# Moving the later attention loads to GpSimd's queue and attention's result copies and stores to ScalarE

## The chip, the cores and the metric

The kernel runs on one core of one Trainium2 chip. The metric is the device time of one execution in microseconds, the median of several runs. The kernel before has 885.93 us (three runs, 885.02 to 886.97).

## What is computed

Attention with fixed masks, then two chains of matrix products over its 2304 rows:

```python
# q, k, v: 4 batches x 8 heads x 576 positions x 64, float32
scores = (q @ k^T) / 8
# heads 0-3: a key counts if 0 <= i - j < 32
# heads 4-7: a key counts if 0 <= i - j < 128 and (i - j) % 4 == 0
attn = softmax(where(mask, scores, -1e9))
x  = (attn @ v) laid out as 2304 x 512
y  = ((x @ w1) * (x @ w2)) @ w3 @ w_out          # 512 -> 1024 -> 1024 -> 512
z  = (silu(y @ w_gate) * (y @ w_val)) @ w_out2    # 512 -> 1536 -> 512
```

## The kernel before

**Pairs and units.** The 8 heads of a batch are taken two at a time, so there are 16 pairs, four to a batch (pair 0 to 3 is batch 0). A pair's attention is seven units: `scores(i, g)` for two halves of its nine blocks of 64 queries (matmuls L319, mask L333, maximum L336, exponentials on ScalarE L338, normalisation L341 to L343 on VectorE), `transposes(i, g)` for three groups of blocks (L356, copied out of PSUM by ScalarE, L358), and `values(i, g)` for two halves (L371). The halves of a pair use two PSUM banks, `bk6` and `bk7`, once the first weights are folded.

**Loads of a pair.** `load_q` (L296, two DMAs), `load_k` (L299) and `load_v` (L304) bring a pair's inputs. q and k have two buffers: those of pair i+2 are issued when `scores(i, 1)` is done. v has one buffer: that of pair i+1 is issued when `values(i, 1)` is done. In the kernel before, SyncE (SP) issues all of them.

**Weights.** A block of two weight tiles, 1 MB, is loaded by SP into one of three raw buffers (`raw<-w_in`, L155), turned into float32 by ScalarE (L200) and VectorE (L201, L202), and split into a high and a low part (L195 on ScalarE, L196 on VectorE). A raw buffer can be loaded again when L196 has read it. From chunk 0 on, weights of the last stage are converted in the same way by `quarters()` (L514, L515), and stored by SP to DRAM as `wd` and `wod` (L552).

**Chunks.** The first chain works on five chunks of rows (512, 512, 512, 512, 256). Chunk 0 takes attention's result of batch 0 straight from PSUM (L164, L165). The others are read back from DRAM: `values` of pairs 4 to 15 copies its two halves into an output buffer `o0` or `o1`, the first half with ScalarE (L394), the second with VectorE (L396), and SP stores it to `x1d` (L397). The chunk is then loaded as a 1 MB block (`raw<-x1d`, also L155) and split (L164, L165). Inside a chunk, `gate_a` (bank `bk4`, copied to `ta` by L236), `gate_b` (bank `bk5`, L242, split into `p`) and `contract` (banks `bk0` to `bk3`) run for eight slices, and `drain` copies the four banks out (L259 on ScalarE, L261 on VectorE, the same buffers `o0` and `o1`) and stores them from ScalarE's queue (`x2d<-o`, L262). Attention of batch c+1 is spread among the slices of chunk c. All matmuls of a product come as three, L217 to L219 (high by high, high by low, low by high). After chunk 4 comes the last stage (from about 437 us), which has no attention in it.

**Order.** A scheduler decides where the instructions of these pieces stand on each engine from the program and its own estimate of durations; on an engine they then run in that order, and so do the DMAs of one queue.

The lines that decide which queue and engine is used are these:

```python
nc.sync.dma_start(out=ks[i % 2][:, WIN:], in_=k_in[i])                   # load_k, L299
nc.vector.tensor_copy(place(o), src)                                     # second half of a pair's result, L396
nc.sync.dma_start(out=x1d[hp, :, b * S:(b + 1) * S], in_=o)              # its store, L397
```

Of the kernel before, what the change touches and what calls it, by code (L numbers as in the profile page):

```python
# [14 lines left out]
AF = mybir.ActivationFunctionType  # L15
# [3 lines left out]
B, H, S, D = 4, 8, 576, 64  # L19
# [5 lines left out]
WIN = 32  # L25
DIL = 4
NPAIR = H // 2
NP = B * NPAIR
QB = 64
KW = QB + WIN  # L30
# [58 lines left out]
def moe_chain_kernel(tc, q_in, k_in, v_in, w_in, mask_in, out):  # L89
    nc = tc.nc  # L90
# [7 lines left out]
    with static as st, other as ot, psum as pp, dram as dp:  # L98
# [14 lines left out]
        x1d = dp.tile([KT, P, NT], F32, name="x1d")  # L113
# [7 lines left out]
        i = N_W1  # L121
# [41 lines left out]
        def to_parts(src, hi, lo):  # L163
            nc.scalar.activation(hi, src, AF.Copy)  # L164
            return nc.vector.tensor_tensor(out=lo, in0=src, in1=hi.bitcast(F32), op=ALU.subtract)  # L165
# [106 lines left out]
        with att1_pool as a1, att2_pool as a2:  # L272
# [3 lines left out]
            ks = [a1.tile([P, WIN + S], F32, name=f"k{i}") for i in range(2)]  # L276
            vv = a1.tile([P, NBLK, P], F32, name="v")
# [10 lines left out]
            def q_halves(q, j):  # L288
                h = slice(j * D, (j + 1) * D)
                z = q[h].rearrange("d (n z r) -> d n z r", z=2, r=2 * QB)  # L290
                return h, z[:, :, j], z[:, :, 1 - j]

            def load_q(i):
                for j in range(2):
                    h, dst, _ = q_halves(qd[i % 2], j)
                    nc.sync.dma_start(out=dst, in_=q_in[i, h].rearrange("d (n r) -> d n r", r=2 * QB))  # L296

            def load_k(i):
                nc.sync.dma_start(out=ks[i % 2][:, WIN:], in_=k_in[i])  # L299

            def load_v(i):
                src = v_in[i]
                win = bass.AP(tensor=src.tensor, offset=src.offset, ap=[[P, KW], [QB * P, NBLK], [1, P]])
                nc.sync.dma_start(out=vv[:KW], in_=win)  # L304


            att_banks = batt + acc[2:]
# [1 line left out]
            def att_bank():  # L309
                count["att"] += 1  # L310
                return att_banks[count["att"] % len(att_banks)]

            def scores(i, g):
# [33 lines left out]
                if g == 1:  # L347
                    if i + 2 < NP:
                        load_q(i + 2)
                        load_k(i + 2)  # L350
# [9 lines left out]
            def values(i, g):  # L360
                b, hp = divmod(i, NPAIR)

                half = S // 2 if hp >= NPAIR // 2 else 5 * QB
                a, e = (0, half) if g == 0 else (half, S)
                ps = att_bank()
                for n in range(NBLK):
                    lo, hi = max(n * QB, a), min((n + 1) * QB, e)
                    if lo >= hi:
                        continue
                    for j in range(2):  # L370
                        nc.tensor.matmul(  # L371
                            ps[j * D:(j + 1) * D, lo - a:hi - a],
                            vv[:KW, n, j * D:(j + 1) * D],
                            pt[:KW, n, (j + n) % 2 * QB + lo - n * QB:(j + n) % 2 * QB + hi - n * QB],
                            start=True, stop=True,
                        )
                src = ps[:, :e - a]
                if hp >= NPAIR // 2:
                    src = src.rearrange("p (c j) -> p c j", c=2)

                    def place(t):
                        return t.rearrange("p (j c) -> p c j", c=DIL)[:, 2 * g:2 * g + 2]
                else:

                    def place(t):
                        return t[:, a:e]

                if b:

                    if g == 0:  # L390
                        count["o"] += 1
                    o = ost[count["o"] % len(ost)]
                    if g == 0:
                        nc.scalar.activation(place(o), src, AF.Copy)  # L394
                    else:
                        nc.vector.tensor_copy(place(o), src)  # L396
                        nc.sync.dma_start(out=x1d[hp, :, b * S:(b + 1) * S], in_=o)  # L397
                elif hp >= NPAIR // 2:
                    cut = CMAX // DIL
                    parts = [xb[0][:, w, hp].rearrange("p (j c) -> p c j", c=DIL)[:, 2 * g:2 * g + 2] for w in range(2)]  # L400
                    to_parts(src[:, :, :cut], *parts)
                    nc.vector.tensor_copy(xr.rearrange("p (j c) -> p c j", c=DIL)[:, 2 * g:2 * g + 2], src[:, :, cut:])
                else:
                    cut = min(e, CMAX)
                    to_parts(src[:, :cut - a], *[xb[0][:, w, hp, a:cut] for w in range(2)])
                    if e > cut:
                        nc.vector.tensor_copy(xr, src[:, cut - a:])
                if b == 0 and g == 1:
                    nc.sync.dma_start(out=x1d[hp, :, CMAX:S], in_=xr)
                if g == 1 and i + 1 < NP:  # L410
                    load_v(i + 1)
# [3 lines left out]
            for i in range(NP):  # L415
                if i + 1 < NP:
                    units += [(scores, i + 1, g) for g in range(2)]
                units += [(transposes, i, g) for g in range(3)]
                units += [(values, i, g) for g in range(2)]
                done_at.append(len(units))  # L420
# [22 lines left out]
            for kk in ks:  # L443
                nc.gpsimd.memset(kk[:, 0:WIN], 0.0)
            make_identity(nc, ident)
            load_k(0)
            load_q(0)
            load_block()
            nc.sync.dma_start(out=mask[:, :2], in_=mask_in[:, :2])
            load_block()  # L450
            load_k(1)
            load_q(1)
            load_v(0)
            load_block()
            nc.sync.dma_start(out=mask[:, 2:], in_=mask_in[:, 2:])
# [8 lines left out]
            for s in range(2 * K1):  # L464
                h, j = divmod(s, K1)
# [386 lines left out]
```

## Time and profile before

| what | us |
|---|---|
| median of three runs | 885.93 |
| the profiled execution's own time | 883.1 |
| its span, first to last instruction | 881.3 |
| TensorE (PE) matmuls busy | 850.6, 97% of the span |
| VectorE (DVE) busy | 595.5, 68% |
| ScalarE (ACT) busy | 350.5, 40% |
| GpSimd (POOL) busy | 3.2 |

The span is what the profiler shows instruction by instruction; the time of the execution is 1.8 us longer. An idle time is listed with the engine and line that ended it. Matmul ends are modelled, so that a matmul's listed duration overlaps the next one's. "SPq" and "ACTq" are the instructions by which an engine issues a DMA. The granted clock of TensorE (PEclk) is given as a share of 2.4 GHz.

### The profile page before, as it was taken

The numbers are of one execution on the slowest core, as the hardware profiler recorded it, in microseconds if no ns is written. First come the engines' busy times: TensorE is split into PE (matmuls) and PEld (weight loads), VectorE is DVE, ScalarE is ACT, GpSimd is POOL, SyncE is SP. The second block draws the span as 40 slices with busy tenths as digits, with TensorE's granted clock in tenths as the row PEclk, the third lists the DMA queues.
The fourth block names the chain that finished last, engine by engine and source line by source line (L and its number), as shares of the span: only waits on it lengthen the run. The fifth ranks groups of instructions, "written<-read, shape, count | busy, mean of one in ns | idle before, by whom it ended". The sixth has DMA issues, their size and how long they took to land.

```text
span 881.3 us, 13296 instructions
## 1 busy us (share of the span) xinstructions
PE 850.6 (97%) x5065; PEld 774.9 (88%) x5066; DVE 595.5 (68%) x1105; ACT 350.5 (40%) x809; POOL 3.2 (0%) x12
## 2 busy tenths in 40 slices
PE   7699899979999999999899999999999999999998
PEld 5478788857888788888899999999999999999998
DVE  6788957447645672465667776798766686666666
ACT  5786854445544552444453222242222132222221
POOL 1000000000000000000000000000000000000000
PEclk9799999989999999999999999999999999999999
DMA  9988738574874667467799666678766667766312
GB/s 282 266 279 273 251 117 267 168 239 124 277 227 141 220 210 262 159 206 248 245 369 372 215 211 201 196 269 263 226 205 214 203 205 248 241 205 213 120 48 73
DMA packets 92432, 192.95 MB, mean 219 GB/s; under 512 B 6480, under 2 KB 56272, under 8 KB 87632
## 3 DMA queue, kind: packets, MB, share of 16 engines
q1 hardware_dynamic: 89488, 187.37, 65.2%
q10 hardware_dynamic: 2880, 4.72, 1.5%
q8 instruction: 40, 0.66, 0.3%
q14 instruction: 24, 0.20, 0.1%
HBM read 150.65 MB, written 41.42 MB: 218 GB/s over the span
## 4 chain that ended last, share of the span: by engine, by line
PE 50%; DMA 13%; DVE 4%; ACT 3%; issue 2%; SPq 0%; ACTq 0%; DVEq 0%
PE bk L217 17%; PE bk L219 17%; PE bk L218 17%; DMA raw<-w_in 6%; DMA wd<-stage 3%; DMA wd<-mid 1%; DMA raw<-x1d 1%; DMA x1d<-o 1%; DVE mid L515 1%; DVE stage L515 1%; DVE x L165 1%; ACT mid L514 1%; ACT s L338 1%; DVE p L165 0%; ACT raw L200 0%
## 5 line engine op out<-in xcount | busy, mean ns | idle before, releaser
L705 DVE TENSOR_TENSOR s<-bk,s 128x384 f32<-128x384 f32 x252 | 137.7, 554 | 52.4 <-PE bk L219 31.5
L217 PE MATMUL bk<-x,w 128*128 128x512 f32 (+2 forms) x368 | 137.3, 374 | 7.6 <-ACT x L164 3.9
L218 PE MATMUL bk<-x,w 128*128 128x512 f32 (+2 forms) x368 | 136.7, 372 | 0.1
L219 PE MATMUL bk<-x,w 128*128 128x512 f32 (+2 forms) x368 | 136.0, 369 | 0.0
L219 PE MATMUL bk<-p,wo 128*128 128x384 f32 x288 | 97.3, 338 | 0.0
L217 PE MATMUL bk<-p,wo 128*128 128x384 f32 x288 | 96.8, 337 | 0.0
L218 PE MATMUL bk<-p,wo 128*128 128x384 f32 x288 | 96.8, 336 | 0.0
L747 DVE TENSOR_TENSOR acc<-bk,acc 128x384 f32<-128x384 f32 x120 | 66.5, 554 | 44.7 <-PE bk L219 44.3
L708 ACT ACTIVATE s<-s 128x384 f32<-128x384 f32 x72 | 37.6, 525 | 129.0 <-DVE s L705 127.9
L217 PEld LDWEIGHTS bk<-x,w 128*128 128x128 f32 x368 | 70.1, 191 | 18.3 <-ACT ta L236 4.6
L218 PEld LDWEIGHTS bk<-x,w 128*128 128x128 f32 x368 | 70.5, 192 | 9.9 <-DVE x L165 0.5
L219 PEld LDWEIGHTS bk<-x,w 128*128 128x128 f32 x368 | 70.5, 191 | 9.8
L164 ACT ACTIVATE p<-s 128x384 fp32r<-128x384 f32 x72 | 37.7, 526 | 101.6 <-DVE s L709 101.6
L217 PE MATMUL bk<-w 128*128 128x384 f32 (+1 forms) x196 | 70.7, 365 | 3.9 <-ACT w L195 3.9
L218 PE MATMUL bk<-w 128*128 128x384 f32 (+1 forms) x196 | 70.3, 360 | 0.0
L218 PE MATMUL bk<-w,mid 128*128 128x384 f32 x204 | 68.6, 336 | 0.0
L200 ACT ACTIVATE raw<-raw 128x1024 f32<-128x1024 f32 (+1 forms) x39 | 44.2, 1133 | 60.4 <-DMA raw<-w_in 60.2
L219 PE MATMUL bk<-w 128*128 128x384 f32 (+1 forms) x196 | 68.0, 361 | 0.0
L219 PE MATMUL bk<-w,mid 128*128 128x384 f32 x204 | 67.9, 337 | 0.0
L217 PE MATMUL bk<-w,mid 128*128 128x384 f32 x204 | 67.8, 336 | 0.0
L218 PE MATMUL bk<-p,W 128*128 128x512 f32 (+1 forms) x160 | 59.3, 375 | 0.0
L219 PE MATMUL bk<-p,W 128*128 128x512 f32 (+1 forms) x160 | 58.8, 372 | 0.0
(99 smaller groups left out, 1603.4 us busy)
## 6 DMA issues: line engine op xcount, KB each, us to landing
raw<-w_in SPq DMA_DIRECT2D x37, 1024.0 KB, 7.2
mid<-wd SPq DMA_DIRECT2D x72, 512.0 KB, 4.2
w<-wd SPq DMA_DIRECT2D x45, 512.0 KB, 3.5
wo<-wod SPq DMA_DIRECT2D x36, 512.0 KB, 4.7
wd<-stage SPq DMA_DIRECT2D x16, 896.0 KB, 6.0
wd<-mid SPq DMA_DIRECT2D x8, 896.0 KB, 5.4
v<-v_in SPq DMA_DIRECT2D x16, 432.0 KB, 4.7
q<-q_in SPq DMA_DIRECT2D x32, 160.0 KB, 5.3
```

What stands on the lines that cost most here:

```text
L164: nc.scalar.activation(hi, src, AF.Copy)
L165: return nc.vector.tensor_tensor(out=lo, in0=src, in1=hi.bitcast(F32), op=ALU.subtract)
L200: nc.scalar.activation(hi.bitcast(F32), hi.bitcast(F32), AF.Prelu, scale=REBIAS, alpha=SIGN_UP)
L217: nc.tensor.matmul(ps, wh, xh, start=start, stop=False)
L218: nc.tensor.matmul(ps, wh, xl, start=False, stop=False)
L219: nc.tensor.matmul(ps, wl, xh, start=False, stop=stop)
L338: nc.scalar.activation(s[:, n], s[:, n], AF.Exp, bias=m[:, 0, n:n + 1], accum_out=m[:, 1, n:n + 1])
L514: nc.scalar.activation(dst[:, :, 0], src, AF.Copy)
L515: nc.vector.tensor_tensor(out=dst[:, :, 1], in0=src, in1=dst[:, :, 0].bitcast(F32), op=ALU.subtract)
L705: nc.vector.tensor_tensor(out=dst[m], in0=x[m], in1=y[m], op=ALU.add)
L708: nc.scalar.activation(u[0], u[0], AF.Silu)
L747: nc.vector.tensor_tensor(out=a, in0=ps, in1=a, op=ALU.add)
```

## The change

The loads of q, k and v of pairs 4 to 15 are issued by GpSimd. The second half of a pair's result is copied by ScalarE as well, and ScalarE's queue stores it to `x1d`. SP keeps the weights, the loads of pairs 0 to 3, the stores of converted weights and the loads from DRAM.

```diff
             def load_q(i):
                 for j in range(2):
                     h, dst, _ = q_halves(qd[i % 2], j)
-                    nc.sync.dma_start(out=dst, in_=q_in[i, h].rearrange("d (n r) -> d n r", r=2 * QB))
+                    (nc.sync if i < NPAIR else nc.gpsimd).dma_start(out=dst, in_=q_in[i, h].rearrange("d (n r) -> d n r", r=2 * QB))
 
             def load_k(i):
-                nc.sync.dma_start(out=ks[i % 2][:, WIN:], in_=k_in[i])
+                (nc.sync if i < NPAIR else nc.gpsimd).dma_start(out=ks[i % 2][:, WIN:], in_=k_in[i])
 
             def load_v(i):
                 src = v_in[i]
                 win = bass.AP(tensor=src.tensor, offset=src.offset, ap=[[P, KW], [QB * P, NBLK], [1, P]])
-                nc.sync.dma_start(out=vv[:KW], in_=win)
+                (nc.sync if i < NPAIR else nc.gpsimd).dma_start(out=vv[:KW], in_=win)
...
                     if g == 0:
                         nc.scalar.activation(place(o), src, AF.Copy)
                     else:
-                        nc.vector.tensor_copy(place(o), src)
-                        nc.sync.dma_start(out=x1d[hp, :, b * S:(b + 1) * S], in_=o)
+                        nc.scalar.activation(place(o), src, AF.Copy)
+                        nc.scalar.dma_start(out=x1d[hp, :, b * S:(b + 1) * S], in_=o)
```

The scheduler's order changes with it. Three places show how.

SP in the start-up, from v of pair 1 on (`q_100` and `k_102` are the buffers of pair 4, `raw_109` is the third raw buffer). Before:

```order
L304 DMA v<-v_in 96x9x128
L296 DMA q_100<-q_in 64x5x128 x2
L155 DMA raw_109<-w_in 128x2048
L299 DMA k_102<-k_in 128x576
L409 DMA x1d<-xr 128x64
L155 DMA raw_78<-w_in 128x2048
```

And in the changed kernel:

```order
L304 DMA v<-v_in 96x9x128
L155 DMA raw_109<-w_in 128x2048
L409 DMA x1d<-xr 128x64
L155 DMA raw_78<-w_in 128x2048
```

The three loads of pair 4 are now the first DMAs on GpSimd's queue; v of pair 1 stays on SP.

ScalarE at the end of chunk 0, where pair 7 ends (its result is in `o0`, its second half in `bk6`; `bk0` and `bk2` are chunk 0's drain). Before:

```order
L394 ACTIVATE o0_80<-bk7_89 128x2x144
L259 ACTIVATE o1_81<-bk0_82 128x512
L262 DMA x2d_91<-o1_81 128x512
L259 ACTIVATE o1_81<-bk2_84 128x512
L262 DMA x2d_91<-o1_81 128x512
L358 ACTIVATE pt_112<-bk7_89 96x384
```

And in the changed kernel:

```order
L394 ACTIVATE o0_80<-bk7_89 128x2x144
L259 ACTIVATE o1_81<-bk0_82 128x512
L262 DMA x2d_91<-o1_81 128x512
L259 ACTIVATE o1_81<-bk2_84 128x512
L396 ACTIVATE o0_80<-bk6_88 128x2x144
L262 DMA x2d_91<-o1_81 128x512
L397 DMA x1d_90<-o0_80 128x576
L358 ACTIVATE pt_112<-bk7_89 96x384
```

The copy and the store of pair 7 now stand behind the drain's second copy into `o1` and behind the issue of its store.

TensorE at the start of chunk 1 (`x_67` is chunk 1's operand, `q_100` and `k_102` are now pair 10, `pt` and `v` pair 8). Before:

```order
L371 MATMUL bk_88<-pt,v 64x64 x10
L371 MATMUL bk_89<-pt,v 64x64 x8
L217 MATMUL bk_86<-x_67,w 128x512
L217 MATMUL bk_87<-x_67,w 128x512
L319 MATMUL bk_88<-k_102,q_100 128x96 x3
L218 MATMUL bk_86<-x_67,w 128x512
```

And in the changed kernel:

```order
L371 MATMUL bk_88<-pt,v 64x64 x10
L371 MATMUL bk_89<-pt,v 64x64 x8
L319 MATMUL bk_88<-k_102,q_100 128x96 x5
L217 MATMUL bk_86<-x_67,w 128x512
L217 MATMUL bk_87<-x_67,w 128x512
L319 MATMUL bk_89<-k_102,q_100 128x96 x4
L218 MATMUL bk_86<-x_67,w 128x512
```

Five blocks of pair 10's scores moved ahead of the first product with chunk 1's operand, and the other four blocks, which need `bk7` (`bk_89`) free, stand right behind that product.

## Rows read from the trace of the kernel before

**Rows 1.** The page, busy time, share of the span and instructions of each engine
```profile
PE 850.6 (97%) x5065; PEld 774.9 (88%) x5066; DVE 595.5 (68%) x1105; ACT 350.5 (40%) x809; POOL 3.2 (0%) x12
```

**Rows 2.** Stretches: length, busy time (instructions) of each engine, PEclk, DMA share, GB/s
```profile
26.00:41.00 15.00, 6.71 (x33) 4.85 (x32) 11.34 (x23) 10.00 (x28) 0.00 (x0) 0.66 1.03 281
95.00:102.50 7.50, 4.96 (x21) 4.13 (x22) 6.96 (x12) 4.02 (x7) 0.00 (x0) 0.77 0.88 288
179.00:195.00 16.00, 9.83 (x96) 7.92 (x95) 8.87 (x17) 7.38 (x25) 0.00 (x0) 0.79 0.83 264
```

**Rows 3.** Waits of TensorE's matmuls: waited for, us in total, times, longest
```profile
PE bk L217 <- ACT x L164: 3.9, 2, 2.4
PE bk L217 <- ACT ta L236: 3.8, 3, 2.5
PE bk L371 <- ACT pt L358: 3.1, 1, 3.1
```

**Rows 4.** Waits of SP's queue, same columns
```profile
SPq L304 <- PE bk L371: 64.6, 14, 8.1
SPq L155 <- DVE w L196: 37.3, 12, 7.7
```

**Rows 5.** Timeline, 84 to 99 us, VectorE and SP: start, duration, instruction
```profile
96.37 1.22 DVE L196 TENSOR_TENSOR w<-raw,w 128x1024 fp32r<-128x1024 f32 x1
...
97.62 0.33 SPq L155 DMA_DIRECT2D raw<-w_in  x1
```

**Rows 6.** Timeline, 24 to 46 us, SP and one TensorE wait
```profile
25.30 0.33 SPq L304 DMA_DIRECT2D v<-v_in  x1
26.35 1.52 SPq L296 DMA_DIRECT2D q<-q_in  x2
...
30.78 0.42 SPq L299 DMA_DIRECT2D k<-k_in  x1
...
35.81 0.91 PE L371 MATMUL bk<-pt,v 96*64 96x64 f32 x12 [1.88 <-DMA v<-v_in]
```

**Rows 7.** Timeline, 179 to 191 us, all engines, in brackets idle time and what ended it
```profile
179.59 2.25 PE L319 MATMUL bk<-k,q 128*128 128x96 f32 x18
179.70 0.33 SPq L304 DMA_DIRECT2D v<-v_in  x1
179.76 0.67 DVE L396 COPY o<-bk 128x288 f32<-128x288 f32 x1 [5.23 <-issue]
180.50 0.33 SPq L397 DMA_DIRECT2D x1d<-o  x1
180.64 0.60 ACT L259 ACTIVATE o<-bk 128x512 f32<-128x512 f32 x1 [2.40 <-DMA x2d<-o]
...
184.34 0.39 SPq L155 DMA_DIRECT2D raw<-x1d  x1
...
186.90 1.45 PE L371 MATMUL bk<-pt,v 96*64 96x64 f32 x36 [3.10 <-ACT pt L358]
...
190.79 1.22 PE L217 MATMUL bk<-x,w 128*128 128x512 f32 x2 [2.44 <-ACT x L164]
```

**Rows 8.** DMA issues: names, queue, times, KB each, median us from issue to landing
```profile
v<-v_in SPq DMA_DIRECT2D x16, 432.0 KB, 4.7
...
x2d<-o ACTq DMA_DIRECT2D x16, 256.0 KB, 2.0
x1d<-o SPq DMA_DIRECT2D x12, 288.0 KB, 3.7
```

**Rows 9.** Waits of ScalarE, columns as in Rows 3
```profile
ACT stage L514 <- DMA wd<-stage: 15.9, 7, 3.7
```

**Rows 10.** Groups of VectorE's instructions: the copy's busy us, mean ns, idle before it
```profile
L396 DVE COPY o<-bk 128x256 f32<-128x256 f32 (+1 forms) x12 | 6.5, 544 | 17.5 <-ACT ta L236 7.3 <-issue 5.2 <-PE bk L371 4.9
```

**Rows 11.** Timeline, pair 15: its v on SP, and its first values matmuls
```profile
326.52 0.34 SPq L304 DMA_DIRECT2D v<-v_in  x1
...
337.05 0.78 PE L371 MATMUL bk<-pt,v 96*64 96x64 f32 x20
```

## The prediction

> **What bounds the kernel.** I read the busy times first: TensorE is busy for 97% of the span [rows 1], so that the change can only pay in the few gaps of TensorE before attention ends, and can only cost by making new ones. The stretches show where those gaps are: about 8 us in the 15 us around 33 us, 2.5 us around 99 us, and 6 us of the 16 us between 179 and 195, each with the granted clock at 0.66 to 0.79, a mix of the 2.4 and the 1.2 GHz level [rows 2]. Nothing else that the change touches leaves TensorE idle for more than about a microsecond. The waits of TensorE say what ended the gaps: ScalarE's split of a chunk's operand, `ta`, and ScalarE's copies of transposed scores [rows 3].
>
> SP's queue looks far worse. It stands for 64.6 us in front of loads of v, waiting for the values matmuls that free their buffer [rows 4]. That is the wait which the change takes away, so the question is who stood behind it. The weight loads also wait, 37.3 us, but for VectorE's L196, which frees the raw buffer [rows 4]. One example: L196 ends at 96.37 + 1.22 = 97.59, the load is issued at 97.62 [rows 5]; a free SP queue would have issued it no earlier. So most of SP's waiting is in front of work that had no buffer anyway.
>
> **The change, part by part.** The sum is made against the profiled execution (883.1 us); the median of the runs stands 2.8 us above it, and the total is added to the median.
>
> A. Start-up. q and k of pair 4, 2 x 160 and 288 KB by their shapes, leave SP's queue, where they were issued behind v of pair 1 [rows 6]. TensorE waits 1.88 us for this v, until 35.81 [rows 6], while the DMA engines are full and move 281 GB/s [rows 2]. On a queue of their own the 608 KB (0.62 MB) can be carried beside v and the weight load ahead of it: 0.62 MB / 281 GB/s = 2.2 us that these may lose. The lower bound is 0, if GpSimd's loads start late enough to come behind them anyway. Part of a loss is taken back in the gap around 99 us, where ScalarE's split is awaited [rows 2, 3]. I take +0.6, bounds 0 to +2.2.
>
> B. Start of chunk 0 (95 to 102 us). The order on VectorE and ScalarE changes by one L196 or so among the splits that TensorE awaits. One of them is 1.22 us [rows 5]. I take 0, bounds -1.2 to +1.2.
>
> C. Start of chunk 1. This is the longest chain that the change enters. Before, pair 7's second half is copied at 179.76, stored at 180.50, the chunk's load is issued at 184.34 when the store has landed (3.84 us later), and TensorE starts on it at 190.79 [rows 7]. Now the copy stands behind the drain's L259, which waits 2.40 us for a store and ends at 181.24; the copy (0.67), one issue (0.33) and its own issue bring the store to 182.25, 1.75 us later. In return it leaves SP's queue, where v with 432 KB was issued 0.80 us ahead of it [rows 7]. ScalarE's stores of similar size land in 2.0 us, SP's in 3.7 [rows 8]. With 2.0 us the load is issued at 184.25 (-0.1), with 3.84 at 186.1 (+1.75); I take the middle, +0.8. Against it, five of pair 10's blocks of scores, ten matmuls, now fill the gap: 18 took 2.25 us [rows 7], so ten are 1.25 us less to do afterwards. The other four blocks wait for the copy of pair 8's second half, which now stands on ScalarE behind the split of the operand, and that gives some of it back; I count 0.8 of the 1.25. Net 0, bounds -1.4 to +3.0 (store late, and a microsecond or so of waiting for that copy).
>
> A rule speaks against C's better half. The Trainium skill, "DMA: Bandwidth & Descriptors", section "Issuing engines are not separate DMA queues", says that DMAs started from several engines share the same 16 DMA engines, and that starting them from several saves only the sequencer's issue time. By that rule the store would land as late as before, C would be +0.95, D below nothing, and the sum +1.85, 887.8 us; the landing times of the two queues speak against it here [rows 8].
>
> D. Converted weights. ScalarE waits 15.9 us in seven places for a stage buffer's store to land [rows 9]; these stores share SP's queue with v and `x1d`. Of TensorE's wait for `ta`, 3.8 us, the longest, 2.5, lies where attention is over; at most the other 1.3 us hang on this [rows 3]. I take -0.4, bounds -1.3 to 0.
>
> E. ScalarE gets twelve copies and twelve issues, VectorE loses the copies: 12 x (0.544 + 0.33) = 10.5 us [rows 7, 10]. ScalarE is idle for 60% of the span [rows 1], which hides it, unless `ta` or `p` is queued behind a copy that waits for values matmuls. Some wait of this kind will appear; the nearest row is the present wait for `ta`, about 1.3 us each [rows 3]. I take +0.3, bounds 0 to +2. VectorE's relief I cost at nothing: the waits of rows 3 are for ScalarE, not for VectorE.
>
> F. GpSimd's loads: 12 v, 24 q and 12 k move. No DMA of GpSimd is in the trace, so its latency is unknown; SP's v lands in 4.7 us [rows 8]. The tightest v is that of pair 8, issued 179.70 and needed at 186.90, 7.2 us [rows 7]; pair 15 has 10.5 us [rows 11]. Even the first may be late without cost: its values need 1.45 us and must end by 190.79, so a landing of 9.6 us is hidden. Bounds are 0 up to twice today's 4.7; for three times see below. I take 0. On GpSimd's queue a load waits only behind older loads whose release comes earlier.
>
> Sum: +0.6 + 0 + 0 - 0.4 + 0.3 = +0.5 us, so 883.6 for an execution like the profiled one, 886.4 for the median.
>
> **Rivals.**
>
> *The shorter queues pay.* The `x1d` store lands in 2.0 us, the fill works fully, the stage stores come early and chunk 0 gains its 1.2 us, with nothing lost in the start-up: -1.4 - 1.3 - 1.2 = -3.9, 882.0 us. For it: the two queues' landings [rows 8], and a shorter gap at 179 also shortens the time at the lower clock. Against: the copy now waits behind the drain [rows 7].
>
> *The start-up pays for it.* GpSimd's q and k start before v of pair 1 has landed, take their share, and TensorE's wait at 35.81 grows by the full 2.2 us [rows 2, 6], with no gap to take it back: 888.1 us, slower. It decides as soon as those 608 KB begin to move before about 33 us. The Trainium skill, "DMA: Bandwidth & Descriptors", section "Queues, rings and completion order", has each DMA engine take turns between the queues with work, at packets. By that rule this is what happens; no row here shows two loading queues side by side. Against: the gap around 99 us waits for ScalarE and VectorE [rows 2, 3].
>
> *GpSimd's loads are slow.* With three times today's landing, 14.1 us, v of pair 8 is there at 193.8 and its values end at 195.2 instead of before 190.8 (+4.5), and v of pair 15 comes at 340.6 instead of 337.05 (+3.6) [rows 7, 11]: +8.1, 894 us. It starts to cost from 9.6 us on. The Trainium skill, "SBUF — State Buffer", section "SBUF: two separate sides", says GpSimd cannot write the descriptors of its DMAs while VectorE works in a two-port mode; no run here shows it yet.
>
> **Numbers.** The forecast gets 0.50, the gain 0.25, the start-up 0.15, the slow loads 0.08, and 0.02 is left for something slower. A measurement of this kernel can tell about 0.2%, 1.8 us, from no change. Of the forecast's 0.50, 0.33 lies within that, 0.07 below, 0.10 above, since its own range with about half of the bounds is 884 to 890. The gain adds 0.24 faster and 0.01 same; the start-up 0.13 slower and 0.02 same; the rest 0.10 is slower. That is 0.31, 0.36 and 0.33. The range goes from 881.5, just under the gain, to 891.5, and leaves out the slow loads and the tails.
>
> **What would show it.** Right: TensorE's gap between 179 and 195 still there within a microsecond or two, SP's waits before L304 and L296 mostly gone without the weight loads' issues moving against L196, `x1d` stores landing in 2 to 3 us, v still landing within 9 us. Wrong: a longer wait for v at 36 us that the later gaps don't absorb; TensorE waiting for v of any pair from 4 on; ScalarE's `ta` late behind a copy; or chunk 1 starting more than 2 us sooner.

## The result, and the profile after

The changed kernel takes 890.95 us (median of 20 runs, 885.76 to 897.61), the kernel before 885.05 (20 runs, 882.76 to 888.93): a ratio of 1.0067, 95% interval 1.0049 to 1.0085, some 5.9 us slower. Ratios here are estimated from fast executions alone; a single execution was a slow one (895.80 us, with q and k of pairs 4 and 6 on SP), which that run's median includes. The profiled execution took 892.0 us, its span is 890.2 (881.3 before). TensorE's mean granted clock is 0.979 of full speed, 0.984 before.

The page's busy times, which answer to [rows 1]:

```profile
PE 852.6 (96%) x5066; PEld 776.9 (87%) x5066; DVE 591.2 (66%) x1093; ACT 356.9 (40%) x821; POOL 37.7 (4%) x60
```

TensorE works 2.0 us more than in [rows 1] and is idle 6.9 us more (37.6 against 30.7). ScalarE got its 6.4 us and paid nothing visible for them. The waits of TensorE's matmuls, against [rows 3]:

```profile
PE bk L217 <- ACT x L164: 10.0, 3, 5.6
...
PE bk L371 <- DMA v<-v_in: 3.9, 1, 3.9
PE bk L371 <- ACT pt L358: 3.1, 1, 3.1
PE bk L217 <- ACT ta L236: 2.2, 2, 1.5
```

The wait for the split operand `x` went from 3.9 to 10.0 us, that for v of pair 1 from 1.88 [rows 6] to 3.9; `pt` is as it was, and `ta` lost 1.6. SP's waits, against [rows 4]:

```profile
SPq L155 <- DVE w L196: 60.6, 14, 7.4
...
SPq L155 <- DMA x1d<-o: 49.0, 3, 29.0
...
SPq L304 <- PE bk L371: 11.7, 3, 5.5
```

SP stands 11.7 us in front of loads of v, those of pairs 1 to 3, where it stood 64.6, and it stands the longer in front of loads whose buffer or data is not there. No weight load was issued earlier for it by more than 0.2 us, as expected.

Three stretches of the timeline show the loss, the start-up, the start of chunk 0 and that of chunk 1; the first and the last answer to [rows 6] and [rows 7]:

```profile
25.47 0.33 SPq L304 DMA_DIRECT2D v<-v_in  x1
26.80 1.70 POOL L296 DMA_DIRECT2D q<-q_in  x2 [22.89 <-PE bk L319]
...
28.50 0.58 POOL L299 DMA_DIRECT2D k<-k_in  x1
...
37.89 0.91 PE L371 MATMUL bk<-pt,v 96*64 96x64 f32 x12 [3.88 <-DMA v<-v_in]
...
98.32 1.16 ACT L195 ACTIVATE w<-raw 128x1024 fp32r<-128x1024 f32 x1 [0.35 <-DVE raw L202]
...
99.35 1.17 ACT L200 ACTIVATE raw<-raw 128x1024 f32<-128x1024 f32 x1
...
100.38 1.12 ACT L164 ACTIVATE x<-bk 128x256 fp32r<-128x256 f32 x2
...
101.56 0.73 PE L217 MATMUL bk<-x,w 128*128 128x512 f32 x2 [3.92 <-ACT x L164]
...
187.11 0.88 POOL L304 DMA_DIRECT2D v<-v_in  x1 [13.34 <-PE bk L371]
187.26 0.68 ACT L396 ACTIVATE o<-bk 128x288 f32<-128x288 f32 x1
187.40 0.33 ACTq L262 DMA_DIRECT2D x2d<-o  x1
187.98 0.33 ACTq L397 DMA_DIRECT2D x1d<-o  x1
...
189.43 1.34 POOL L296 DMA_DIRECT2D q<-q_in  x2 [1.45 <-PE bk L319]
...
193.27 0.38 SPq L155 DMA_DIRECT2D raw<-x1d  x1
...
196.12 0.88 POOL L304 DMA_DIRECT2D v<-v_in  x1 [4.79 <-PE bk L371]
202.74 2.00 ACT L164 ACTIVATE x<-raw 128x1024 fp32r<-128x1024 f32 x2 [7.29 <-DMA raw<-x1d]
...
203.84 1.22 PE L217 MATMUL bk<-x,w 128*128 128x512 f32 x2 [5.64 <-ACT x L164]
```

The rows of the kernel before for the start of chunk 0, and for the landing of chunk 1's load, are these:

```profile
92.86 1.18 ACT L200 ACTIVATE raw<-raw 128x1024 f32<-128x1024 f32 x1
93.91 1.18 ACT L195 ACTIVATE w<-raw 128x1024 fp32r<-128x1024 f32 x1
94.98 1.09 ACT L164 ACTIVATE x<-bk 128x256 fp32r<-128x256 f32 x2
...
96.12 0.73 PE L217 MATMUL bk<-x,w 128*128 128x512 f32 x2 [1.44 <-ACT x L164]
...
189.68 2.00 ACT L164 ACTIVATE x<-raw 128x1024 fp32r<-128x1024 f32 x2 [2.83 <-DMA raw<-x1d]
```

In the start-up v of pair 1 is issued at the same time as before and used 2.1 us later. Before chunk 0 TensorE waits 3.92 us for the split of `x`, where it waited 1.44. ScalarE has two pieces of weight blocks (L195, L200) just ahead of the split, but it had two before as well (L200, L195): the order changed, not the amount. At chunk 1 two things grew. The store of pair 7 is issued at 187.98 and the chunk's load 5.29 us later, at 193.27 (3.84 in [rows 7]); and the load is there after 9.47 us (202.74), where it took 5.34 (184.34 to 189.68). The stretches, in which the load's time is cut in three, against [rows 2] (length, busy time and instructions of PE, PEld, DVE, ACT, POOL, granted clock, DMA share, GB/s):

```profile
28.00:43.00 15.00, 6.65 (x29) 4.77 (x30) 11.70 (x23) 8.59 (x26) 1.07 (x2) 0.59 0.91 250
100.00:107.50 7.50, 4.06 (x15) 3.44 (x16) 6.14 (x11) 3.42 (x5) 0.00 (x0) 0.66 0.91 331
186.00:207.00 21.00, 11.68 (x105) 9.95 (x105) 8.00 (x16) 8.34 (x27) 3.66 (x5) 0.70 0.61 186
...
193.27:198.65 5.38, 4.16 (x46) 3.80 (x46) 2.43 (x7) 1.16 (x4) 0.88 (x1) 0.62 0.91 272
198.70:201.00 2.30, 0.00 (x0) 0.00 (x0) 0.00 (x0) 0.00 (x0) 0.00 (x0) 0.50 0.65 190
201.00:202.70 1.70, 0.00 (x0) 0.00 (x0) 0.00 (x0) 0.00 (x0) 0.00 (x0) 0.50 0.08 28
```

For 5.38 us the DMA engines are full, and at 198.65 all but one of the 16 have finished their share of the load. In the last 1.7 us the DMA share is 0.08, little more than one engine of 16, and every compute engine stands still for it, with TensorE's clock at its lower level, 0.50.

What the DMAs took, against [rows 8]:

```profile
v<-v_in POOLq DMA_DIRECT2D x12, 432.0 KB, 5.6
...
x1d<-o ACTq DMA_DIRECT2D x12, 288.0 KB, 4.5
```

The store to `x1d` lands in 4.5 us from ScalarE's queue; it was 3.7 from SP's.

### The profile page after: what moved, and what is told of

Same layout as the page of the kernel before. It is cut to its first block, busy times and chain, and to the rows that moved or that the text cites. A ratio compares the mean times of both kernels' runs of the same rounds, so it can differ in the third digit from the quotient of the medians.

```text
span 890.2 us, 13289 instructions
## 1 busy us (share of the span) xinstructions
PE 852.6 (96%) x5066; PEld 776.9 (87%) x5066; DVE 591.2 (66%) x1093; ACT 356.9 (40%) x821; POOL 37.7 (4%) x60
## 4 chain that ended last, share of the span: by engine, by line
PE 82%; DMA 12%; DVE 4%; ACT 2%; issue 1%; SPq 0%; ACTq 0%
PE bk L217 25%; PE bk L218 25%; PE bk L219 25%; DMA raw<-w_in 7%; PE bk L319 2%; PE bk L371 2%; DMA raw<-x1d 2%; DMA v<-v_in 1%; PE bk L356 1%; DMA x1d<-o 1%; DVE w L196 1%; DVE raw L202 1%; DMA wd<-mid 1%; ACT raw L200 1%; DVE x L165 0%
## 5 line engine op out<-in xcount | busy, mean ns | idle before, releaser
L217 PE MATMUL bk<-x,w 128*128 128x512 f32 (+2 forms) x368 | 136.3, 372 | 12.2 <-ACT x L164 10.0
L219 PE MATMUL bk<-x,w 128*128 128x512 f32 (+2 forms) x368 | 135.7, 369 | 0.0
L219 PE MATMUL bk<-p,wo 128*128 128x384 f32 x288 | 97.3, 338 | 0.0
L217 PE MATMUL bk<-p,wo 128*128 128x384 f32 x288 | 96.9, 337 | 0.0
L747 DVE TENSOR_TENSOR acc<-bk,acc 128x384 f32<-128x384 f32 x120 | 66.5, 554 | 44.2 <-PE bk L219 43.8
L217 PEld LDWEIGHTS bk<-x,w 128*128 128x128 f32 x368 | 69.5, 190 | 23.0 <-ACT x L164 10.8
L219 PEld LDWEIGHTS bk<-x,w 128*128 128x128 f32 x368 | 69.8, 190 | 9.6
L217 PE MATMUL bk<-w 128*128 128x384 f32 (+1 forms) x196 | 70.7, 365 | 4.4 <-ACT w L195 4.4
L242 DVE TENSOR_TENSOR ta<-bk,ta 128x512 f32<-128x512 f32 (+1 forms) x40 | 25.4, 635 | 68.4 <-PE bk L219 54.3
L219 PE MATMUL bk<-w 128*128 128x384 f32 (+1 forms) x196 | 68.6, 364 | 0.0
L219 PE MATMUL bk<-w,mid 128*128 128x384 f32 x204 | 67.9, 337 | 0.0
L217 PE MATMUL bk<-w,mid 128*128 128x384 f32 x204 | 67.8, 336 | 0.0
L200 ACT ACTIVATE raw<-raw 128x1024 f32<-128x1024 f32 (+1 forms) x39 | 44.4, 1138 | 53.3 <-DMA raw<-w_in 53.0
L219 PE MATMUL bk<-p,W 128*128 128x512 f32 (+1 forms) x160 | 59.1, 373 | 0.0
```

Of the source, the lines that this page charges most:

```text
L200: nc.scalar.activation(hi.bitcast(F32), hi.bitcast(F32), AF.Prelu, scale=REBIAS, alpha=SIGN_UP)
L217: nc.tensor.matmul(ps, wh, xh, start=start, stop=False)
L219: nc.tensor.matmul(ps, wl, xh, start=False, stop=stop)
L242: nc.vector.tensor_tensor(out=u, in0=bb[:, :n], in1=ta[:, :n], op=ALU.mult)
L747: nc.vector.tensor_tensor(out=a, in0=ps, in1=a, op=ALU.add)
```

## The experiments

Two theories. **Queues:** a load on a queue of its own shares the DMA engines with the load that TensorE awaits, where on SP it stood behind it; the loss sits where TensorE waits for a load. **Results:** the copy and the store on ScalarE are late at chunk 1. Rivals to both: the **order** of the instructions, which the scheduler changed along with the queues, and **chance** in one profile. Ratios are against runs of the kernel before on the same chip (medians 883.98 to 884.64); a per cent is 8.8 us. A ratio is an estimate of its own, not the quotient of the two medians, and differences in us are worked out from it.

### The changed kernel again

No edit.

> The changed kernel once more, for a second profile. Each place of the loss should return if it belongs to the change: theory 'queues' (a load on a queue of its own takes from the loads that TensorE awaits): about 5.9 us slower than before (+0.67%), TensorE's wait for v near 38 us again about 4 us (1.9 before), and the gap before chunk 1's first product again 5 to 6 us. Rival 'chance' (one DMA engine that ran late in that one profile: the chunk's load had 15 of its 16 shares there after 5.4 us and the last after 9.4): the median is the same, but the gap before chunk 1 is back to 2 to 3 us.

892.18 us, ratio 1.0081 (1.0050 to 1.0112). TensorE waits 3.7 us for v, and at chunk 1:

```profile
187.20 0.33 ACTq L397 DMA_DIRECT2D x1d<-o  x1
...
192.28 0.38 SPq L155 DMA_DIRECT2D raw<-x1d  x1
...
204.30 1.22 PE L217 MATMUL bk<-x,w 128*128 128x512 f32 x2 [7.24 <-ACT x L164]
```

The gap is larger still (7.24), the store again takes 5.08 us, the load 10.9. So neither is the chance of one profile. The gap before chunk 1 is above the 5 to 6 us of the expectation. The wait for `x` before chunk 0 did not come back: 1.9 us, after 3.92 in the first profile.

### Loads alone

```diff
-                        nc.scalar.activation(place(o), src, AF.Copy)
-                        nc.scalar.dma_start(out=x1d[hp, :, b * S:(b + 1) * S], in_=o)
+                        nc.vector.tensor_copy(place(o), src)
+                        nc.sync.dma_start(out=x1d[hp, :, b * S:(b + 1) * S], in_=o)
```

(against the changed kernel)

> Only the loads of pairs 4 to 15 go to GpSimd; copies and stores stay on VectorE and SP. Theory 'queues': the start-up and the start of chunk 0 carry the loss, so +4 to +5 us against before, with the wait for v near 38 us at 3.5 to 4 us. Rival 'results' (copy behind the drain and the store carry the loss): within 1 us of before.

888.65 us, ratio 1.0041 (1.0017 to 1.0066), 3.6 us slower. The wait for v is 3.9 us, and chunk 1 starts in good time: the store lands in 2.9 us, with v no longer ahead of it on SP, and the gap is 1.7. The chunk's load takes 8.1 us.

```profile
184.82 0.32 SPq L397 DMA_DIRECT2D x1d<-o  x1
...
187.73 0.38 SPq L155 DMA_DIRECT2D raw<-x1d  x1
...
196.92 1.22 PE L217 MATMUL bk<-x,w 128*128 128x512 f32 x2 [1.70 <-ACT x L164]
```

### Results alone

```diff
-                        nc.vector.tensor_copy(place(o), src)
-                        nc.sync.dma_start(out=x1d[hp, :, b * S:(b + 1) * S], in_=o)
+                        nc.scalar.activation(place(o), src, AF.Copy)
+                        nc.scalar.dma_start(out=x1d[hp, :, b * S:(b + 1) * S], in_=o)
```

(against the kernel before)

> Only the second halves' copies and stores go to ScalarE; all loads stay on SP. Theory 'queues': the order up to chunk 1 is that of before, so nothing until 180 us, then the copy behind the drain, about +1.4 us at the start of chunk 1, in all +1 to +2. Rival 'results': +4 to +6, with the gap before chunk 1 at 5 to 6 us.

886.32 us, ratio 1.0017 (0.9998 to 1.0037): 1.5 us, which does not stand clear of nothing. The store from ScalarE's queue lands in 3.73 us (184.21 to 187.94), as from SP before, although v of pair 8 (on SP) and the drain's store are issued 1.1 and 0.6 us ahead of it. The chunk's load takes 8.6 us (5.34 before) and the gap is 3.2, with every load on SP.

### Only q and k of pair 4

```diff
-                    nc.sync.dma_start(out=dst, in_=q_in[i, h]...)
+                    (nc.sync if i != 4 else nc.gpsimd).dma_start(out=dst, in_=q_in[i, h]...)
-                nc.sync.dma_start(out=ks[i % 2][:, WIN:], in_=k_in[i])
+                (nc.sync if i != 4 else nc.gpsimd).dma_start(out=ks[i % 2][:, WIN:], in_=k_in[i])
```

> The kernel before, with nothing but q and k of pair 4 (two times 160 KB and 288 KB) moved to GpSimd; TensorE's, VectorE's and ScalarE's orders are those of before. Theory 'queues' (the rival 'the start-up pays' of the prediction): TensorE's wait for v of pair 1 grows from 1.9 to about 4 us and the median by about 2 us. Rival 'order' (the start-up's delay comes from elsewhere, or is taken back in the gap around 99 us): within 0.7 us of before.

887.65 us, ratio 1.0038 (1.0019 to 1.0056): three DMAs on another queue cost 3.4 us, with every compute engine's order unchanged.

```profile
28.07 1.48 POOL L296 DMA_DIRECT2D q<-q_in  x2 [24.16 <-PE bk L319]
...
39.72 0.91 PE L371 MATMUL bk<-pt,v 96*64 96x64 f32 x12 [4.57 <-DMA v<-v_in]
```

This is the clearest finding of the study. GpSimd's q and k, issued 1.3 to 2.8 us behind v of pair 1, land ahead of it, at 36.98, 37.88 and 39.38 us against 39.59; in the kernel before, on one queue, v lands first, at 35.67, and they at 36.45 to 40.19. In the seven profiles of this study with q and k of pair 4 on GpSimd the wait for v is 2.5 to 4.6 us, in the six with these and v of pair 1 on SP 1.0 to 2.2.

### Only q and k of pair 6

The same edit with `i != 6`.

> The kernel before, with nothing but q and k of pair 6 on GpSimd. That alone makes the scheduler give VectorE and ScalarE the changed kernel's order between 85 and 110 us (each weight block's L200/L202 one place ahead of the block before's L195/L196). Theory 'order': TensorE's gap before chunk 0's first product grows as in the changed kernel, from 1.6 to 3 or 4 us, and the median by about 3 us (+2 to +4). Rival 'queues only' (the start of chunk 0 was late because of the loads beside it, v of pair 5 and q, k of pair 4): within 1 us of before, since only 0.6 MB move queue here and long before 99 us.

886.35 us, ratio 1.0020 (0.9997 to 1.0043): 1.8 us, which does not stand clear of nothing either. In the profile the wait before chunk 0's first product is 3.2 us (1.4 before), as the order theory has it. But two kernels whose order there is that of before wait 4.1 and 3.7 us in their profiles (the change from chunk 1 on only, and all three places), so this wait does not tell the two orders apart. And GpSimd issues these loads at 81.8 and 83.4 us, and they then move beside weight blocks, so the run doesn't part the order from the sharing.

### The changed kernel with q and k of pairs 4 and 6 on SP

```diff
-(nc.sync if i < NPAIR else nc.gpsimd).dma_start(...)
+(nc.gpsimd if i > 4 and i != 6 else nc.sync).dma_start(...)
```

(in `load_q` and `load_k`)

> The changed kernel with q and k of pairs 4 and 6 back on SP: the start-up's queue is as before, and the order up to chunk 0 is that of before. Theory 'start-up plus order': both places are mended, about 5 us less than the changed kernel, so +0.5 to +2 against before, what is left being the start of chunk 1. Rival 'chunk 1' (most of the loss is the late store and chunk load there): still +4 or more.

890.83 us, ratio 1.0046 (1.0014 to 1.0079). The wait for v is back at 1.7 us, but the time is still 4.1 us above before. That is the rival's number, though the interval (1.2 to 7.0) reaches down to the theory's; chunk 1 waits 5.8 us.

### Only v of pair 1

```diff
-                nc.sync.dma_start(out=vv[:KW], in_=win)
+                (nc.gpsimd if i == 1 else nc.sync).dma_start(out=vv[:KW], in_=win)
```

> The kernel before, with nothing but v of pair 1 on GpSimd, the load that TensorE waits for near 36 us; every engine's order is that of before. Theory 'queues' turned round (a load on its own queue overtakes what is queued ahead of it on SP): v lands 3 us or more earlier, the wait of 1.9 us is gone, and the median falls by 1 to 2 us. Rival 'bandwidth' (the engines are full, so what v gains the weight blocks behind it lose, and TensorE waits for L195 instead): within 0.7 us of before.

884.80 us, ratio 1.0005 (0.9987 to 1.0023): no difference, the bandwidth rival.

```profile
27.05 0.98 POOL L304 DMA_DIRECT2D v<-v_in  x1 [23.13 <-PE bk L371]
...
36.87 0.91 PE L371 MATMUL bk<-pt,v 96*64 96x64 f32 x12 [1.51 <-ACT w L195]
```

On a queue of its own v lands 9.7 us after its issue, hardly sooner than from SP (10.5 to its use in [rows 6]), and the 1.5 us that are left are a wait for a weight's L195 instead.

### The store on SP, the copy on ScalarE

```diff
-                        nc.scalar.dma_start(out=x1d[hp, :, b * S:(b + 1) * S], in_=o)
+                        nc.sync.dma_start(out=x1d[hp, :, b * S:(b + 1) * S], in_=o)
```

> The changed kernel with the copies on ScalarE but the stores to x1d on SP's queue. Theory 'store' (on ScalarE's queue the store stands behind the drain's x2d store and lands in 5.1 to 5.3 us, on SP alone in about 3): chunk 1's load is issued 2 us earlier, and the median is 1 to 2 us below the changed kernel, +4 to +5.5 against before. Rival 'load' (what is late is the chunk's load, whatever the store): the store's landing falls, but the time stays within 0.8 us of the changed kernel.

889.62 us, ratio 1.0063 (1.0039 to 1.0088), as the changed kernel.

```profile
184.58 0.33 ACTq L262 DMA_DIRECT2D x2d<-o  x1
185.15 0.32 SPq L397 DMA_DIRECT2D x1d<-o  x1
...
190.34 0.38 SPq L155 DMA_DIRECT2D raw<-x1d  x1
...
199.66 2.00 ACT L164 ACTIVATE x<-raw 128x1024 fp32r<-128x1024 f32 x2 [6.62 <-DMA raw<-x1d]
```

The store takes 5.19 us from SP's queue too. The theory "store" falls: it is not the queue that makes it late. v of pair 8 and the drain's 256 KB start just ahead of it, but so they do in "Results alone", where it lands in 3.73 us with v on SP. So it was late where the copy behind the drain and v on GpSimd's queue came together; how they make it late is not shown.

### The change from chunk 1 on only

q and k from pair 12 (`i > 11`), v from pair 10, results from pair 9.

```diff
-                        nc.vector.tensor_copy(place(o), src)
-                        nc.sync.dma_start(out=x1d[hp, :, b * S:(b + 1) * S], in_=o)
+                        nc.scalar.activation(place(o), src, AF.Copy) if i > 8 else nc.vector.tensor_copy(place(o), src)
+                        (nc.scalar if i > 8 else nc.sync).dma_start(out=x1d[hp, :, b * S:(b + 1) * S], in_=o)
```

> The change only where the three costly places are past: q and k from pair 12, v from pair 10, results from pair 9 on. Up to chunk 1's first product the kernel is that of before. Theory 'places' (start-up, start of chunk 0 and start of chunk 1 carry the whole loss, and from there on the change gains about 2 us): 1 to 2 us faster than before (-0.1 to -0.2%). Rival 'no gain' (the 2 us after chunk 1 are chance of the profiled runs): within 0.7 us of before.

884.91 us, ratio 1.0010 (0.9990 to 1.0030): no difference. All of the loss but at most 2.7 us is made before chunk 1's first product, and behind it no gain is seen.

### Pair 7's result as before

The same edit to the changed kernel, with `i != 7`.

> The changed kernel, but pair 7's second half is copied by VectorE and stored by SP as before; all loads stay on GpSimd. Theory 'copy behind the drain' (the drain's x2d store, 256 KB, starts ahead of the x1d store and both with v of pair 8): the store lands in about 3 to 4 us instead of 5.1 to 5.3, the gap before chunk 1 falls from 6 or 7 us to 3 or 4, and the time by 2 to 3 us against the changed kernel (+3 to +4.5 against before). Rival 'loads beside it' (GpSimd's q, k and v alone make store and chunk load late): store 5 us, gap 5 us or more, time unchanged.

889.88 us, ratio 1.0079 (1.0050 to 1.0109).

```profile
184.06 0.32 SPq L397 DMA_DIRECT2D x1d<-o  x1
...
187.50 0.38 SPq L155 DMA_DIRECT2D raw<-x1d  x1
...
196.34 1.22 PE L217 MATMUL bk<-x,w 128*128 128x512 f32 x2 [3.49 <-ACT x L164]
```

In the profile the theory holds: the store lands in 3.44 us, the load in 7.7, the wait falls to 3.5. In the time nothing is gained: 7.0 us above before (4.4 to 9.6), where the theory had 3 to 4.5.

### v of pair 9 on SP

```diff
-                (nc.sync if i < NPAIR else nc.gpsimd).dma_start(out=vv[:KW], in_=win)
+                (nc.gpsimd if i > 3 and i != 9 else nc.sync).dma_start(out=vv[:KW], in_=win)
```

> The changed kernel with one DMA moved: v of pair 9 back on SP, behind the chunk's load instead of beside it; all engines' orders stay. Theory 'v beside the chunk's load' (in four profiles of the combination the load's last share came 4 to 5.6 us after its eighth): the load lands in 5.5 to 8 us instead of 9.3 to 10.9, the gap before chunk 1 is 3 to 4 us, and the time 1.5 to 3 us below the changed kernel. Rival 'the load is late anyway' (q and k of pair 11 ahead of it, or TensorE's instruction fetch that falls into it): landing 9 us or more, time unchanged.

893.14 us, ratio 1.0098 (1.0063 to 1.0134).

```profile
190.16 0.38 SPq L155 DMA_DIRECT2D raw<-x1d  x1
...
197.66 2.00 ACT L164 ACTIVATE x<-raw 128x1024 fp32r<-128x1024 f32 x2 [5.08 <-DMA raw<-x1d]
...
198.77 1.22 PE L217 MATMUL bk<-x,w 128*128 128x512 f32 x2 [3.69 <-ACT x L164]
```

Again the profile does what the theory says, one DMA less beside the load and the load lands in 7.5 us; and again the time does not follow (8.7 us above before). This profiled execution took 887.2 us, the shortest of six that go up to 897.5.

### All three places at once

q and k of pairs 4 and 6 and v of pair 9 on SP, pair 7's result as before (the edits above together).

> The changed kernel with all three places mended at once: q and k of pairs 4 and 6 and v of pair 9 on SP, pair 7's second half copied and stored as before; the other loads and results stay moved. Theory 'three places' (start-up, order before chunk 0, start of chunk 1 carry the loss): within 1.5 us of before, the stretch from the first weights to 57 us back at about 45, 175 to 215 at 40 to 42. Rival 'every loss sits elsewhere too' (the moved queues make other loads late in ways that single profiles don't show): still +4 or more in the median.

890.04 us, ratio 1.0070 (1.0042 to 1.0098). The rival's number. The stretch at chunk 1 is mended in part (102.4 us in the table below, 100.0 before), and the start-up was slow in this profile although its queues are those of before.

### Where the time lies

For all profiles I cut TensorE's time at the same work: every kernel has 4008 product matmuls (L217 to L219), and the cuts are the starts of the 1st, 84th, 185th, 266th, 563rd and 1605th, which in the kernel before lie at 12.3, 57, 87, 115, 215 and 460 us. Each column is the time between two cuts, in us; ahead of and behind them all kernels agree within 1.1.

| kernel | to 57 | 57-87 | 87-115 | 115-215 | 215-460 |
|---|---|---|---|---|---|
| before | 44.75 | 30.23 | 27.82 | 100.04 | 244.91 |
| only v of pair 1 | 45.07 | 30.37 | 28.05 | 100.16 | 242.60 |
| only q, k of pair 6 | 44.24 | 30.20 | 30.91 | 100.42 | 244.30 |
| late only | 46.37 | 29.58 | 29.61 | 100.76 | 242.85 |
| results alone | 47.46 | 30.07 | 28.76 | 102.88 | 242.31 |
| only q, k of pair 4 | 48.15 | 31.33 | 27.31 | 102.07 | 242.76 |
| loads alone | 46.97 | 30.51 | 30.42 | 101.74 | 242.91 |
| after | 47.30 | 30.54 | 31.88 | 105.32 | 241.44 |
| after, again | 47.21 | 31.34 | 29.73 | 106.23 | 241.48 |
| store on SP | 45.91 | 30.70 | 30.06 | 104.78 | 242.43 |
| pairs 4, 6 on SP | 44.55 | 33.82 | 29.56 | 105.38 | 242.90 |
| pair 7 as before | 44.95 | 30.40 | 30.77 | 102.54 | 243.63 |
| v of pair 9 on SP | 46.86 | 29.84 | 30.56 | 102.67 | 242.15 |
| three places | 47.66 | 30.23 | 29.09 | 102.36 | 244.40 |

- *To 57.* The column scatters by 3 us even where nothing of it was changed (44.2 to 47.7), so a single profile proves little here; the wait for v and the time of the pair-4 run carry the case. The seven kernels with pair 4 on GpSimd have a mean of 46.8, the others of 45.7.
- *87 to 115.* The seven kernels with the changed order of weight blocks lie at 29.7 to 31.9, the seven with the order of before at 27.3 to 29.6. The means, 30.6 and 28.6, are 2.0 us apart, and q and k of pair 6 alone make the step. Only 0.35 of the 2.0 lies ahead of chunk 0's first product, where the split is awaited; the rest lies behind it. The kernels with three places or with pairs 4 and 6 mended have other loads on GpSimd there and stay below 29.6.
- *115 to 215.* Neither half of the change: 100.0 to 102.1 (the highest is pair 4 alone). Results alone 102.9, loads alone 101.7. Both: 104.8 to 106.2, about 5 us above the first four rows' mean of 100.3, where the two halves add 2.5 and 1.4, in one profile each. Either mending brings it to 102.4 to 102.7.
- *215 to 460.* The full change takes 241.4 to 242.9; the four first rows 242.6 to 244.9. A gain of 1 to 2 us at best, and the run that has only this part shows none.

## Why the prediction was right in its range and wrong in its forecast

890.95 us lies inside the range (881.5 to 891.5), near its upper end. The likeliest case, no measurable change at 886.4, did not happen; the measured sign had 0.33. That the range holds the number is in part luck: no case that the prediction worked out comes to it, the start-up rival giving 888.1 and the slow loads 894. Of its signs of being wrong one came, the longer wait for v that later gaps don't absorb; and of its signs of being right two failed, the gap between 179 and 195 us, which grew by 3.2 us, and the `x1d` stores, which landed in 4.5 us and not in 2 to 3.

**What bounds.** Right: SP's long waits were in front of work without a buffer, and removing them moved no weight load forward (k of pair 4 alone went out earlier, at 28.50 instead of 30.78 us).

**A, start-up, +0.6.** The mechanism was named and the size was too small. v comes 2.0 us later (3.88 against 1.88 us of waiting), and pair 4 alone costs 3.4 us (1.7 to 5.0). The step that failed is "part of a loss is taken back in the gap around 99 us": between 57 and 115 us the pair-4 run takes 58.64 us (31.33 + 27.31) and before 58.05, so in these two profiles nothing is taken back, and the time of the pair-4 run leaves no room for +0.6. This is the mechanism of the rival "the start-up pays" (888.1), which I gave 0.15, and it is shown: GpSimd's q and k move at 28 us, before v is there, and land ahead of it. The Trainium skill, "DMA: Bandwidth & Descriptors", section "Queues, rings and completion order", has the engines take turns between queues at packets; the trace agrees, 3.9 us of waiting with two queues against 1.9 with one, and what was issued behind v on the other queue landed before it.

**B, start of chunk 0, 0.** The bounds of 1.2 were too narrow: 2.0 us by the profiles' means. I had priced one L196 ahead of the split that TensorE awaits; but the wait for the split is 1.9 to 3.9 us in the seven kernels with the new order and 1.1 to 4.1 in the others, and of the 2.0 us only 0.35 lies ahead of chunk 0's first product. Behind it TensorE waits once more, for VectorE's L402 (a copy of attention's result): 1.6 to 2.2 us in the seven, at most 1.6 in the others. It comes with pair 6 on GpSimd; whether by the changed order or by the weight blocks that share the engines with that pair's loads isn't settled, and the time of pair 6 alone (+1.8, -0.3 to +3.8) leaves even the size short of proof.

**C, start of chunk 1, 0.** Wrong, and the largest term in the profiles: about 5 us between 115 and 215 us, where the upper bound was 3.0. Two steps failed. "ScalarE's stores land in 2.0 us" was read as the queue's property; it depended on what moved beside them: in the kernel before, three of them, issued at 178.26, 181.27 and 185.07 us, landed in 2.0, 3.7 and 6.1 us. The store of pair 7 landed in 4.9 to 5.3 us in the five profiles with both the copy behind the drain and v of pair 8 on GpSimd, the same from either queue, and in 2.9 to 3.7 where one of the two was missing. The Trainium skill, "DMA: Bandwidth & Descriptors", section "Issuing engines are not separate DMA queues", stood against this term. The trace agrees with it: 5.29 us from ScalarE, 5.19 from SP. And the sum had no term for the chunk's load at all, which the prediction took to last as long as before; it grew from 5.3 to 9.3 to 10.9 us in four profiles of the combined change. GpSimd's loads move beside it there, but they are not all of it: it took 8.6 us with the results alone and 7.5 with pair 4 alone, where SP issues every load at that time.

**D, converted weights, -0.4.** Of the right size, as far as it shows. ScalarE's wait for stage stores fell from 15.9 us [rows 9] to 7.2:

```profile
ACT stage L514 <- DMA wd<-stage: 7.2, 5, 2.3
```

Little of it was on the path: TensorE's wait for `ta` fell by 1.6 us, 1.0 of it where attention is over (2.48 to 1.48), and the run with the late part alone is no faster.

**E, ScalarE's copies, +0.3.** Hidden, as said. But "the waits of rows 3 are for ScalarE, not for VectorE" holds of the three rows that stand there and not of the trace, in which TensorE also waits 3.8, 2.6 and 1.4 us for VectorE's L165, L407 and L402; these end before 100 us, ahead of the first copy that VectorE loses. **F, GpSimd's loads, 0.** Right as far as v goes: from pair 4 on TensorE never waits for it; it lands in 5.6 us, GpSimd issues it mostly within 0.3 us of its release though an issue takes it 0.87 us and SP 0.33. The rival "GpSimd's loads are slow" fell. What F missed is that a prefetch need not be late to cost something: it only has to move beside a load that is awaited.

**What stays open.** By the measured times the loads carry most of the loss (+3.6 alone, the results +1.5), and most or all of it is made before chunk 1's first product (the late part alone +0.9, -0.9 to +2.7). The three places are seen one by one in profiles, and the first in the time as well, but mending them, singly or together, brought no time clearly below the changed kernel's: +4.1, +5.6, +7.0, +8.7 and +6.2 us against +5.9 and +7.2. Runs of the changed kernel spread over 12 us, of the one before over 6 to 9 (by chip), and the profiled ones of two mended kernels were 2.1 and 5.9 us below their medians. Which loads pay in the longer executions, no profile here shows. That the loss is the sum of the three places is therefore argued, not shown.

## What to carry to other kernels

SP's queue, which stood waiting for buffers, cost nothing here; look at who is late behind such a queue before you spread its loads. On one queue the awaited load, issued first, landed first: moving prefetches to a queue of their own put them beside it and cost 3.4 us for three DMAs, and moving the awaited load instead gained nothing while the DMA engines were full. When a change lets the scheduler reorder, compare the orders before you price the queues; moving one load that triggers the new order, as was done with pair 6, does not part the two.

## What was not expected

**One or two late DMA engines hold everything.** In the changed kernel's two profiles half of the 16 shares of chunk 1's load had landed 5.2 and 5.3 us after the issue, all but one and all but two of them within 5.6 us, and the last 9.4 and 10.9 us; in the kernel before the eighth landed after 5.0 and the last after 5.3. Two kernels with every load on SP there (pair 4 alone, results alone) show the same on a smaller scale: 2.5 and 2.6 us between the eighth and the last share, against 0.4 before. It is 4.0 to 5.6 us in four profiles of both halves (the changed kernel's two, the store on SP, pairs 4 and 6 on SP) and 0.2 to 2.6 in the other ten; so the changed queues go with the worst of it, and don't make all of it. What held the late engines up is not known. This load was as late as its slowest share, and its mean bandwidth does not tell.

**Whether both halves cost more together than apart is open.** Between 115 and 215 us 1.4 and 2.5 us became 5, and the store of pair 7 is late only with both. But each half has one profile, in a stretch that scatters by 2 us without either, and the measured times of the halves (+3.6 and +1.5) nearly add up to that of the whole (+5.9).

**The changed kernel's runs lie further apart.** 885.8 to 897.6 us, and 882.8 to 888.9 before, 20 runs each. That the moved loads do it is not shown: with the loads alone nine runs lie within 7.0 us, and the kernel before on another chip within 9.1 (28 runs).
